# One sum bank at a time in the down phase, and score visits of seven banks

## The chip, the cores and the metric

The kernel runs on one core of a Trainium2 chip. The core has five engines with a queue each: TensorE (PE, matrix products, with weight loads listed apart as PEld), VectorE (DVE), ScalarE (ACT), GpSimd (POOL) and SyncE (SP, which here only issues transfers). An engine takes its instructions in order and waits for the others by semaphores. Products are written to PSUM, which this kernel uses as eight banks of 512 float32 numbers for each of 128 partitions; here ACT and DVE read it, and POOL works on SBUF alone.

The metric is the device time of one execution, in microseconds (us).

## The reference

One layer on 2048 tokens of width 512. Attention and a gated feed-forward part run side by side on the same normalised input, and both are added to it.

```python
xn = _layernorm(x)                                     # [2048, 512]
q, k, v = (xn @ wqkv), split into 32 heads of width 16
scores = q k^T / 4, kept where 0 <= i - j < 256        # sliding window
A = softmax(scores) v, heads joined, @ wo
B = ((xn @ w_gate) * (xn @ w_up)) @ w_down             # hidden width 1792
return x + A + B
```

## The kernel before

**Chunks and stages.** The tokens are worked on in NCH = 4 chunks T of 512 tokens. For a chunk there are the projections (`proj_v`, `proj_qk`), the scores and the values of its attention, the gate and up products of 14 hidden blocks (`gate`, `up`; NF = 14), and the *down phase*: for each of four blocks b of 128 tokens, 14 products of `down` (L432) and four of `wo` (L438) are summed in one PSUM bank `psd`, and `store` (L448) adds them to x on DVE and sends the block out.

**Scores.** Four heads share a group c of 128 columns, as four strips e of 32 rows. A *step* is one entry of the list that `batches` makes: a few pieces (c, key block, first and last query block) that fill 512 columns, for four heads. There are 75 steps: 15 for chunk 0 and 20 for each later chunk, five for each c. `scores` (L317) writes a step into the tile S, four PSUM banks, one bank per head. The four heads use four different 32-row parts of TensorE (`tile_position=(32 * e, 0)`), so that four products run side by side. One ACT instruction (L323) exponentiates the four banks into an SBUF strip P; POOL cuts the far edge of the window out of P (`triangle`, L162), and DVE the near edge (`mask_diag`, L347). S is a single tile: the next step's products wait until the exponential has read it. I call one such excursion of TensorE from the 128-row products to the 32-row products and back a *score visit*.

**Values.** When the strips of a group c are all there, `values` (L370) multiplies them by V in 64 by 32 parts of TensorE into two accumulators, DVE turns them (L376), and `divide` (L385 to L392) divides by the row sums into OT, which `wo` reads.

**Banks.** PSUM is split into S (four banks) and the pool `ps_m` of four one-bank buffers in rotation, which holds everything else: projections, gate, up, accumulators and `psd`. A tile of `ps_m` waits for the reader of the tile four places before it.

**Order.** The order on each engine is written out by `run`. It goes through the 75 steps; after each step's scores it calls `fill`, which issues *fillers* (half a gate, half an up, two down products and so on, from the list made by `fillers`) until a planned amount, `upto`, is spent. The planned amounts rise evenly over all 75 steps, and the table SHIFT moves some of them. Fillers of a chunk T come in this order: gate and up of its first FIRST = 3 blocks, then the down phase of chunk T-1, then the other gates and ups, then the projections of chunk T+1. So the down phase of chunk T-1 is spread over seven steps of chunk T: "score visit, ten to fourteen down products, score visit, ...". PADS puts runs of no-ops between fillers of TensorE at two steps. `norms` (layer norm of chunk T+1, with a transpose by DMA on SP) is hung on five steps at the down phase. Values of two groups are due together at one step; their two divides come 8 and 24 units of spent TensorE time later (`pending`).

Of the kernel before, what the change touches and what calls it, by code (L numbers as in the profile page):

```python
# [24 lines left out]
FIRST = 3  # L25
GAP = 10.6
PAIRS = ((0,), (1,), (2,), (3,)), ((0, 1), (2, 3)), ((0, 1), (2, 3)), ((0, 1), (2,))
SHIFT = {20: -2, 21: -5, 22: -8, 23: -11, 24: -14, 26: -10, 27: -7, 28: -3, 62: 3, 63: 6, 64: 12, 66: 12, 67: 11, 68: 9, 69: 6, 70: 3}
PADS = {27: 120, 57: 146}
MASKED, FIRST_DIVIDE, SECOND_DIVIDE = 8, 8, 24  # L30
COPY = dict(act=2.8, dve=3.2)
EXP, MASK, BOTH, SUMS, DIVIDE, TURN, STATS = 8.7, 1.9, 3.4, 4.2, 8.2, 6.1, 4.2
# [2 lines left out]
class Kernel:  # L35
    def __init__(self, ctx, tc, x, wqkv, wo, wg, wu, wd, out):
        self.ctx, self.tc, self.nc = ctx, tc, tc.nc
        _, S, D = x.shape
        self.S, self.D, self.F = S, D, wg.shape[1]
        assert D == 512 and S % 512 == 0 and self.F % 256 == 0  # L40
        self.NT, self.NCH, self.NF = S // 128, S // 512, self.F // 128
        self.x_d, self.out_d = x.flatten_outer_dims(), out.flatten_outer_dims()
        self.w_d = dict(qkv=wqkv, o=wo, g=wg, u=wu, d=wd)

        def pool(name, bufs, **kw):
            return ctx.enter_context(tc.tile_pool(name=name, bufs=bufs, **kw))
# [79 lines left out]

    def keep_busy(self, n):

        ps = self.ps_m.tile([128, 128], F32, tag="M", name="wps")
        for _ in range(n):  # L130
            self.nc.tensor.matmul(ps[:], lhsT=self.idle[:], rhs=self.idle[:], start=True, stop=True)

# [66 lines left out]
    def norm_transpose(self, t, by_dma):  # L199

        nc = self.nc
        xn = self.xns.pop(t)
        T, b = divmod(t, 4)
        if b == 0:
            self.xnT[T] = self.chunk2.tile([128, 4, 4, 128], BF16, tag="xnT", name=f"xnT{T}")
        if by_dma:
            nc.sync.dma_start_transpose(out=self.xnT[T][:, b, :, :], in_=xn[:])
            return
        n = 2 if b == 0 else 4
        for lo in range(0, 4, n):  # L210
            ps = self.ps_m.tile([128, n, 128], BF16, tag="M", name="xTp")
            for k in range(n):
                nc.tensor.transpose(ps[:, k, :], xn[:, 128 * (lo + k):128 * (lo + k) + 128], self.ident[:])  # L213
            nc.scalar.activation(out=self.xnT[T][:, b, lo:lo + n, :], in_=ps[:], func=ACT.Copy)

    def bank(self, ks, name):

        self.open = 3 not in ks
        if 0 in ks:
            self.cur = self.ps_m.tile([128, 512], F32, tag="M", name=name)  # L220
        return self.cur

    def book(self, engine, took, ready=0):
# [79 lines left out]
                out.append(REST[c])  # L303
        return out

    def scores(self, T, pieces):

        nc = self.nc
        S = self.s_tiles.tile([128, 4, 512], F32, tag="S", name="S")
        P = self.ppool.tile([128, 4, 512], BF16, tag="P", name="P")  # L310
        col = 0
        for c, m, q0, q1 in pieces:
            U, j = divmod(8 * T + m, 8)
            keys, q, n = slice(128 * j, 128 * j + 128), 64 * q0, 64 * (q1 - q0 + 1)
            for e in range(4):
                rows = slice(32 * e, 32 * e + 32)
                nc.tensor.matmul(S[:, e, col:col + n], lhsT=self.K[U, c][rows, keys],  # L317
                                 rhs=self.Q[T, c][rows, q:q + n],
                                 start=True, stop=True, tile_position=(32 * e, 0),
                                 skip_group_check=True)  # L320
            self.parts.setdefault((T, c), []).append((P, col, m, q, n))
            col += n
        nc.scalar.activation(out=P[:, :, 0:col], in_=S[:, :, 0:col], func=ACT.Exp, scale=0.25)  # L323
        self.book("act", EXP)
        self.masked = self.free["act"]
        self.strips[(T, pieces)] = P
        for at in self.places(pieces, 4):
            for half in (slice(0, 64), slice(64, 128)):
                self.triangle(P[half, :, at:at + 64], False)

    def places(self, pieces, far):

# [18 lines left out]
    def values(self, T, c, accs=None):  # L351
# [1 line left out]

        nc = self.nc
        if accs is None:
            accs = [self.ps_m.tile([128, 512], F32, tag="M", name="acc") for _ in range(2)]
# [61 lines left out]
    def down(self, T, b, lo, hi, part=0):  # L418

        nc = self.nc  # L420
        self.open = True
        if lo == 0 and part == 0:
            if T == self.NCH - 1 and b == 3:
                last = self.ps_m.tile([128, 128], F32, tag="M", name="psd3")
                self.sums[b] = [(self.late[3][:, 0:384], 0, 384), (last[:], 384, 512)]
            elif T == self.NCH - 1 and b == 2:
                self.sums[b] = [(self.late[2][:], 0, 512)]
            else:
                self.sums[b] = [(self.ps_m.tile([128, 512], F32, tag="M", name="psd")[:], 0, 512)]
        for f in range(lo, hi):  # L430
            ps, c0, c1 = self.sums[b][part]
            nc.tensor.matmul(ps, lhsT=self.hT[T, f][:, 128 * b:128 * b + 128],  # L432
                             rhs=self.Wd[:, f, c0:c1], start=(f == 0), stop=False)
# [19 lines left out]
    def fillers(self):  # L453
# [54 lines left out]
        for T in range(NCH):  # L508
            if T:
                if T + 1 < NCH:  # L510
                    for i, fs in norms(T + 1, 0, 1).items():
                        self.beside[self.first[T, 0] + (4, 5, 6, 7, 8)[i]] = fs
# [11 lines left out]
        for b in range(4):  # L524
            down(T, b)
            if b < 3:
                wo(T, b, (0, 1, 2))
        return [(*o, None, None)[:4] for o in out]

    def run(self):  # L530
        self.xns, self.stats, self.sums = {}, {}, {}
# [17 lines left out]
        self.beside = {}  # L549
        work = self.fillers()  # L550
        total = sum(w[0] for w in work) - RESERVE + SCORES * len(steps)
        total += sum(VALUES + SECOND * (len(keys) - 1) for keys in due.values())
        spent, n = 0, 0
        self.free = dict(act=0, dve=0)
        valued, ready, pending = -1, -1, []

        def fill(upto, group):
            nonlocal spent, n
            while n < len(work):
# [3 lines left out]
                if spent + cost / 2 > upto and not any(  # L563
                        w[2] is not None and w[2] <= group for w in work[n:]):
                    break
                spent += cost
                self.now = spent
# [10 lines left out]
            self.divide(*key)  # L578
            ready = self.last[key]

        held = None
        for g, s in enumerate(steps):
            keys = due.get(g, [])
            self.pads += PADS.get(g, 0)
            if held is None:
                valued = ready
                fill(-1, g + len(keys) // 2)
                while len(keys) == 2 and self.open:
# [4 lines left out]
            upto = max(total * (g + 1) / len(steps) + SHIFT.get(g, 0), spent + GAP)  # L593
            if g in (1, 2):
                self.new_values()
            for i, key in enumerate(keys):
# [20 lines left out]
        self.ps_s.__exit__(None, None, None)  # L617
        late = self.ctx.enter_context(self.tc.tile_pool(name="ps_late", bufs=1, space=bass.MemoryType.PSUM))
# [16 lines left out]
        self.down(T, 3, 0, self.NF, 1)  # L635
        self.wo(T, 3, (0, 1, 2, 3), 1)
        self.store(T, 3, 1)


@with_exitstack  # L640
# [34 lines left out]
```

## Time and profile before

| | |
|---|---|
| device time, median of three | 263.19 us (263.17 to 263.84) |
| span of the profiled execution, first to last instruction | 261.3 us |
| time around that span (median less span; the profiled execution's own device time is not listed) | 1.9 us |
| busy: PE, DVE, ACT, POOL | 98%, 69%, 67%, 44% of the span |
| mean granted clock of TensorE | 0.999 of full speed |
| stretches with the three down phases | about 69 to 88, 132 to 151 and 195 to 215 us |

Busy time of an engine is the time in which an instruction of it runs. The chain of work that ended last is followed back from the last instruction; its shares say which engine the time goes through. In the lists, `out<-in` are the tiles' names, sizes are partitions x elements, `xN` counts instructions, and a bracket gives the idle time before an instruction and who ended it. Matrix products overlap: each of 128x512 lasts 380 ns in the record, but they start every 216 ns. A few per cent of the products have no record, and where one is missing the trace shows a gap of 0.2 us.

### The profile page before, as it was taken

To read this page: it belongs to the slowest core of one execution; us is meant where nothing else is said; L and a number is where in the kernel's file an instruction comes from. 1 tells how busy PE (TensorE), PEld (TensorE's weight loads), DVE (VectorE), ACT (ScalarE), POOL (GpSimd) and SP (SyncE) were. 2 spreads that over 40 slices of the span, in tenths; PEclk is the share of its full clock that TensorE was granted. 3 is DMA by queue.
4 is the path that set the end of the run, shared out by engine and by line. 5 is a ranking of instruction groups with operands and counts; after the bars stand their busy time and mean duration, and the time that the engine had idled before them with its cause. 6 is when DMAs were issued, how large, how long until landed. Compare 5 with 4: busy or idle time off the path is not lost.

```text
span 261.3 us, 7724 instructions
## 1 busy us (share of the span) xinstructions
PE 255.5 (98%) x3154; PEld 117.4 (45%) x3170; DVE 179.5 (69%) x357; ACT 176.4 (67%) x143; POOL 115.7 (44%) x278
## 2 busy tenths in 40 slices
PE   7999999999999999999999999999999999999995
PEld 7443444444344544344544454344544445444453
DVE  6687888879846597557974769767795235977344
ACT  3477688888757866678775567767787546787600
POOL 6225342425457644334456644544443451464600
PEclk9999999999999999999999999999999999999999
DMA  6999910120012300002001310001000100000002
GB/s 203 373 353 340 284 26 20 24 48 1 3 33 38 94 3 1 3 0 48 3 3 40 83 44 3 0 1 27 24 3 0 43 24 20 5 0 3 1 3 83
DMA packets 19427, 15.05 MB, mean 58 GB/s; under 512 B 7360, under 2 KB 19392, under 8 KB 19392
## 3 DMA queue, kind: packets, MB, share of 16 engines
q1 hardware_dynamic: 18848, 14.26, 18.6%
q8 instruction: 26, 0.43, 0.7%
q10 hardware_dynamic: 544, 0.30, 0.4%
q14 instruction: 9, 0.07, 0.1%
HBM read 9.70 MB, written 2.10 MB: 45 GB/s over the span
## 4 chain that ended last, share of the span: by engine, by line
PE 96%; DVE 1%; DMA 1%; issue 1%
PE gp L399 19%; PE up L410 19%; PE psd L432 17%; PE qkp L255 11%; PE S L317 10%; PE acc L370 7%; PE vp L243 5%; PE psd L438 5%; PE L L432 2%; DMA x<-in_A_x_dram 1%; DVE st L173 1%; PE L L438 1%; PE L L370 0%; PE xTp L213 0%; DVE xn L194 0%
## 5 line engine op out<-in xcount | busy, mean ns | idle before, releaser
L323 ACT ACTIVATE P<-S 128x2048 bf16<-128x2048 f32 x75 | 140.7, 1876 | 49.6 <-PE S L317 41.1
L162 POOL TENSOR_SCALAR_AFFINE_SELECT P<-P 64x256 bf16<-64x256 bf16 x224 | 99.4, 444 | 124.2 <-ACT P L323 109.0
L399 PE MATMUL gp<-xnT,Wg 128*128 128x512 bf16 x224 | 60.1, 380 | 0.0
L410 PE MATMUL up<-xnT,Wu 128*128 128x512 bf16 x224 | 59.1, 380 | 0.0
L415 DVE TENSOR_TENSOR hT<-up,gsb 128x512 bf16<-128x512 f32 x56 | 38.3, 685 | 18.4 <-PE up L410 13.1
L432 PE MATMUL psd<-Wd,hT 128*128 128x512 bf16 (+1 forms) x202 | 46.9, 369 | 0.8 <-issue 0.6
L347 DVE TENSOR_TENSOR P<-P,diag 128x512 bf16<-128x512 bf16 (+1 forms) x75 | 29.6, 394 | 5.9 <-ACT P L323 5.9
L432 PEld LDWEIGHTS <-hT 128*128 128x128 bf16 x238 | 21.3, 98 | 25.3 <-issue 3.5
L410 PEld LDWEIGHTS <-Wu 128*128 128x128 bf16 x224 | 20.4, 98 | 25.6 <-issue 3.3
L399 PEld LDWEIGHTS <-Wg 128*128 128x128 bf16 x224 | 20.3, 98 | 25.3 <-issue 3.3
L317 PE MATMUL S<-Q,K 32*128 32x320 bf16 (+4 forms) x720 | 29.8, 254 | 0.1
L255 PE MATMUL qkp<-xnT,Wqkv 128*128 128x512 bf16 x128 | 29.9, 380 | 0.0
L234 ACT ACTIVATE gsb<-gp 128x512 bf16<-128x512 f32 x38 | 22.3, 596 | 7.7 <-PE gp L399 6.9
L317 PEld LDWEIGHTS <-K 32*128 32x128 bf16 x720 | 10.3, 92 | 30.7 <-issue 30.3
L376 DVE STREAM_TRANSPOSE at<-acc 128x512 f32<-128x512 f32 x30 | 19.1, 688 | 6.5 <-PE acc L370 6.4
L448 DVE TENSOR_TENSOR x<-psd,x 128x512 bf16<-128x512 f32 (+1 forms) x15 | 9.7, 655 | 15.7 <-PE psd L438 15.7
L255 PEld LDWEIGHTS <-Wqkv 128*128 128x128 bf16 x128 | 11.7, 98 | 14.7 <-issue 1.8
L370 PE MATMUL acc<-P,VS 64*32 64x320 bf16 (+4 forms) x672 | 17.7, 253 | 0.0
L370 PE MATMUL acc<-P,V 64*32 64x320 bf16 (+4 forms) x672 | 17.5, 253 | 0.0
L370 PEld LDWEIGHTS <-V 64*32 64x32 bf16 x720 | 15.1, 91 | 2.3 <-issue 1.7
L243 PE MATMUL vp<-Wqkv,xnT 128*128 128x512 bf16 x60 | 14.9, 379 | 0.3 <-issue 0.2
L370 PEld LDWEIGHTS <-VS 64*32 64x32 bf16 x720 | 14.7, 91 | 0.6 <-issue 0.2
(54 smaller groups left out, 178.9 us busy)
## 6 DMA issues: line engine op xcount, KB each, us to landing
out_dram<-x SPq DMA_DIRECT2D x15, 128.0 KB, 1.9
Wg<-in_B_w_gate_dram SPq DMA_DIRECT2D x2, 896.0 KB, 10.9
Wu<-in_B_w_up_dram SPq DMA_DIRECT2D x2, 896.0 KB, 12.4
Wd<-in_B_w_down_dram SPq DMA_DIRECT2D x1, 1792.0 KB, 17.6
Wqkv<-in_A_wqkv_dram SPq DMA_DIRECT2D x3, 512.0 KB, 5.5
x<-in_A_x_dram SPq DMA_DIRECT2D x2, 512.0 KB, 8.3
VS<-V SPq DMA_DIRECT2D x6, 144.0 KB, 2.6
x<-in_A_x_dram SPq DMA_DIRECT2D x3, 256.0 KB, 6.7
```

What stands on the lines that cost most here:

```text
L162: nc.gpsimd.affine_select(out=v, in_=v, pattern=pattern + [[1 if diag else -1, 64]], compare_op=ALU.is_ge if diag else ALU.is_gt, fill=0.0 ...
L234: nc.scalar.activation(out=out, in_=in_, func=ACT.Copy)
L243: nc.tensor.matmul(ps[:], lhsT=self.xnT[T][:, b, k, :], rhs=self.Wqkv[:, k, 1024:1536], start=(k == 0), stop=(k == 3))
L255: nc.tensor.matmul(ps[:], lhsT=self.Wqkv[:, k, lo:lo + 128], rhs=self.xnT[T][:, :, k, :], start=(k == 0), stop=(k == 3))
L317: nc.tensor.matmul(S[:, e, col:col + n], lhsT=self.K[U, c][rows, keys], rhs=self.Q[T, c][rows, q:q + n], start=True, stop=True, tile_posit ...
L323: nc.scalar.activation(out=P[:, :, 0:col], in_=S[:, :, 0:col], func=ACT.Exp, scale=0.25)
L347: self.nc.vector.tensor_tensor(out=v, in0=v, op=ALU.min, in1=self.diag.unsqueeze(1).unsqueeze(1).to_broadcast([128, 4, n, 64]))
L370: nc.tensor.matmul(accs[par][32 * e:32 * e + 32, q:q + n], lhsT=v, rhs=P[rows, e, col:col + n], start=(i == 0), stop=(i == len(todo) - 1), ...
L399: nc.tensor.matmul(ps[:], lhsT=self.Wg[:, k, 128 * f:128 * f + 128], rhs=self.xnT[T][:, :, k, :], start=(k == 0), stop=(k == 3))
L410: nc.tensor.matmul(ps[:], lhsT=self.Wu[:, k, 128 * f:128 * f + 128], rhs=self.xnT[T][:, :, k, :], start=(k == 0), stop=(k == 3))
L415: nc.vector.tensor_tensor(out=self.hT[T, f][:], in0=ps[:], in1=self.gsb[:], op=ALU.mult)
L432: nc.tensor.matmul(ps, lhsT=self.hT[T, f][:, 128 * b:128 * b + 128], rhs=self.Wd[:, f, c0:c1], start=(f == 0), stop=False)
```

## The change

- `ps_m` becomes four pools of one bank each, which `m_tile` takes in turn.
- At three places, after step 2 of the chunks 1, 2 and 3, all PSUM pools are closed and the whole down phase of the chunk before is issued in one piece by the new `down_phase`. The eight banks are then one bank d for the sums of block b, three banks B, and the four banks S. Of b to b + 1, d and B change places at the ends of the four banks (d is bank 3, then 0, then 3, then 0).
- The phase takes seven steps with it (3 to 9 of the chunk). For each b `wide_scores` computes one *plain* step (3, 4, 5, 6) in S, and three of the twelve (step, head) pairs of the steps 7, 8 and 9 in B. The products come in two rounds: first the three pairs in B together with the plain step's head that is *short*, the one that the three pairs leave free, then the plain step's other three heads. B is exponentiated by one or two ACT instructions (a step's heads that lie together), S by one.
- Order within b: BEFORE = 8, 6, 6, 6 down products, the visit, the rest of the down products, `wo`, `store`.
- The fillers ahead of a down phase are all issued before it; the rest is spread evenly over the steps of each stage (`spread`); SHIFT is empty, and PADS moves its second run from step 57 to step 47 and from 146 to 178 no-ops. Pending divides are issued FLUSH = 12 units before the phase. Layer norms of the next chunk come one per b (`along`), and the last at step 11.

```diff
-SHIFT = {20: -2, 21: -5, 22: -8, 23: -11, 24: -14, 26: -10, 27: -7, 28: -3, 62: 3, 63: 6, 64: 12, 66: 12, 67: 11, 68: 9, 69: 6, 70: 3}
-PADS = {27: 120, 57: 146}
+SHIFT = {}
+PADS = {27: 120, 47: 178}
+BEFORE, LEAD, FLUSH = (8, 6, 6, 6), 5, 12
...
-        self.ps_m = pool("ps_m", 4, space=bass.MemoryType.PSUM)
-        self.ps_s = tc.tile_pool(name="ps_s", bufs=1, space=bass.MemoryType.PSUM)
-        self.s_tiles = self.ps_s.__enter__()
+        self.psum = []
+        self.usual_banks(0)
+    def open_banks(self, name, bufs=1):
+        p = self.tc.tile_pool(name=name, bufs=bufs, space=bass.MemoryType.PSUM)
+        self.psum.append(p)
+        return p.__enter__()
+    def close_banks(self, n):
+        for _ in range(n):
+            self.psum.pop().__exit__(None, None, None)
+    def usual_banks(self, at):
+        self.at_bank = at
+        self.m_banks = [self.open_banks(f"ps_m{i}") for i in range(4)]
+        self.s_tiles = self.open_banks("ps_s")
+    def m_tile(self, shape, dtype, name):
+        pool = self.m_banks[self.at_bank]
+        self.at_bank = (self.at_bank + 1) % 4
+        return pool.tile(shape, dtype, tag="M", name=name)
...
+    def score(self, T, pieces, e, bank):
+        out, col, rows = [], 0, slice(32 * e, 32 * e + 32)
+        for c, m, q0, q1 in pieces:
             U, j = divmod(8 * T + m, 8)
-            keys, q, n = slice(128 * j, 128 * j + 128), 64 * q0, 64 * (q1 - q0 + 1)
-            for e in range(4):
-                rows = slice(32 * e, 32 * e + 32)
-                nc.tensor.matmul(S[:, e, col:col + n], lhsT=self.K[U, c][rows, keys],
-                                 rhs=self.Q[T, c][rows, q:q + n],
-                                 start=True, stop=True, tile_position=(32 * e, 0),
-                                 skip_group_check=True)
-            self.parts.setdefault((T, c), []).append((P, col, m, q, n))
+            q, n = 64 * q0, 64 * (q1 - q0 + 1)
+            out.append((col, dict(out=bank[:, col:col + n], lhsT=self.K[U, c][rows, 128 * j:128 * j + 128],
+                                  rhs=self.Q[T, c][rows, q:q + n], tile_position=(32 * e, 0))))
             col += n
-        nc.scalar.activation(out=P[:, :, 0:col], in_=S[:, :, 0:col], func=ACT.Exp, scale=0.25)
-        self.book("act", EXP)
-        self.masked = self.free["act"]
-        self.strips[(T, pieces)] = P
+        return out
+    def score_products(self, work):
+        for _, kw in sorted(work, key=lambda w: w[0]):
+            self.nc.tensor.matmul(kw.pop("out"), start=True, stop=True, skip_group_check=True, **kw)
+    def exp(self, out, in_):
+        self.nc.scalar.activation(out=out, in_=in_, func=ACT.Exp, scale=0.25)
+    def mask_far(self, T, pieces):
+        P = self.strips[(T, pieces)]
         for at in self.places(pieces, 4):
             for half in (slice(0, 64), slice(64, 128)):
                 self.triangle(P[half, :, at:at + 64], False)
+    def scores(self, T, pieces):
+        S = self.s_tiles.tile([128, 4, 512], F32, tag="S", name="S")
+        P, col = self.strip(T, pieces)
+        self.score_products([w for e in range(4) for w in self.score(T, pieces, e, S[:, e])])
+        self.exp(P[:, :, 0:col], S[:, :, 0:col])
+        self.book("act", EXP)
+        self.masked = self.free["act"]
+        self.mask_far(T, pieces)
+    def wide_scores(self, T, pieces, extra, B):
+        S = self.s_tiles.tile([128, 4, 512], F32, tag="S", name="S")
+        short = ({0, 1, 2, 3} - {e for _, e in extra}).pop()
+        work = []
+        for i, (other, e) in enumerate(extra):
+            if (T, other) not in self.strips:
+                self.strip(T, other)
+            work += self.score(T, other, e, B[:, i])
+        work += self.score(T, pieces, short, S[:, short])
+        self.score_products(work)
+        i = 0
+        while i < 3:
+            other, e = extra[i]
+            n = 1
+            while i + n < 3 and extra[i + n][0] == other:
+                n += 1
+            self.exp(self.strips[(T, other)][:, e:e + n, :], B[:, i:i + n, :])
+            i += n
+        P, _ = self.strip(T, pieces)
+        self.score_products([w for e in range(4) if e != short for w in self.score(T, pieces, e, S[:, e])])
+        self.exp(P[:], S[:])
+        self.mask_far(T, pieces)
+        for other in {o: None for o, e in extra if e == 3}:
+            self.mask_far(T, other)
+    def down_phase(self, T, g):
+        s = self.steps
+        plain = [s[g + i][1] for i in range(4)]
+        split = [(s[g + 4 + i][1], e) for i in range(3) for e in range(4)]
+        late, high = None, 0 if self.at_bank == 0 else 1
+        self.close_banks(5)
+        for b in range(4):
+            for name in ("ps_b", "ps_d") if b % 2 != high else ("ps_d", "ps_b"):
+                tiles = self.open_banks(name)
+                if name == "ps_d":
+                    d = tiles.tile([128, 512], F32, tag="d", name="psd")
+                else:
+                    B = tiles.tile([128, 3, 512], F32, tag="B", name="B")
+            self.s_tiles = self.open_banks("ps_s")
+            self.sums[b] = [(d[:], 0, 512)]
+            self.down(T - 1, b, 0, BEFORE[b])
+            for f in self.along.pop((T, b), ()):
+                f()
+            if late:
+                self.mask_diag(T, late)
+            late, extra = plain[b], split[3 * b:3 * b + 3]
+            self.wide_scores(T, late, extra, B)
+            self.down(T - 1, b, BEFORE[b], self.NF)
+            for other, e in extra:
+                if e == 3:
+                    self.mask_diag(T, other)
+            self.wo(T - 1, b, range(4))
+            self.store(T - 1, b)
+            self.close_banks(3)
+        self.usual_banks(0 if high == 0 else 1)
...
+                        if i < 4:
+                            self.along[T, i] = [f for _, f in fs]
+                        else:
+                            self.beside[self.first[T, 0] + 11] = fs
                 gu(T, range(FIRST))
-                for b in range(4):
-                    down(T - 1, b)
-                    wo(T - 1, b, range(4))
-                    add(0, lambda T=T, b=b: self.store(T - 1, b))
+                out.append((None, T))
...
+        downs = {self.first[T, 0] + 3: T for T in range(1, NCH)}
+        def spread(g):
+            end = next((k for k in range(n, len(work)) if work[k][0] is None), len(work))
+            stop = min([k for k in downs if k >= g], default=len(steps))
+            cost = sum(w[0] for w in work[n:end]) - (RESERVE if end == len(work) else 0)
+            cost += SCORES * (stop - g)
+            cost += sum(VALUES + SECOND * (len(due[k]) - 1) for k in due if g <= k < stop)
+            return spent, cost, g, stop - g
...
+            if g in downs:
+                valued = ready
+                fill(10 ** 9, -1)
+                valued = ready
+                assert work[n] == (None, downs[g])
+                late = self.down_phase(downs[g], g)
+                n += 1
+                skip = set(range(g, g + 7))
+                base, cost, g0, count = spread(g + 7)
+                fill(spent + LEAD, -1)
+                self.mask_diag(downs[g], late)
+                continue
...
+            if g + 1 in downs:
+                fill(upto - FLUSH, g)
+                while pending:
+                    pending.pop(0)[1]()
```

More of the change, by code (lines that the diff above doesn't have):

```diff
@@ L127, in keep_busy @@
     def keep_busy(self, n):
-        ps = self.ps_m.tile([128, 128], F32, tag="M", name="wps")
+        ps = self.m_tile([128, 128], F32, "wps")
         for _ in range(n):
@@ L210, in norm_transpose @@
         for lo in range(0, 4, n):
-            ps = self.ps_m.tile([128, n, 128], BF16, tag="M", name="xTp")
+            ps = self.m_tile([128, n, 128], BF16, "xTp")
             for k in range(n):
@@ L219, in bank @@
         if 0 in ks:
-            self.cur = self.ps_m.tile([128, 512], F32, tag="M", name=name)
+            self.cur = self.m_tile([128, 512], F32, name)
         return self.cur
@@ L304, in batches, with strip @@
         return out
-    def scores(self, T, pieces):
-        nc = self.nc
-        S = self.s_tiles.tile([128, 4, 512], F32, tag="S", name="S")
+    def strip(self, T, pieces):
         P = self.ppool.tile([128, 4, 512], BF16, tag="P", name="P")
+        self.strips[(T, pieces)] = P
         col = 0
         for c, m, q0, q1 in pieces:
-            U, j = divmod(8 * T + m, 8)
-            keys, q, n = slice(128 * j, 128 * j + 128), 64 * q0, 64 * (q1 - q0 + 1)
-            for e in range(4):
-                rows = slice(32 * e, 32 * e + 32)
-                nc.tensor.matmul(S[:, e, col:col + n], lhsT=self.K[U, c][rows, keys],
-                                 rhs=self.Q[T, c][rows, q:q + n],
-                                 start=True, stop=True, tile_position=(32 * e, 0),
-                                 skip_group_check=True)
-            self.parts.setdefault((T, c), []).append((P, col, m, q, n))
-            col += n
-        nc.scalar.activation(out=P[:, :, 0:col], in_=S[:, :, 0:col], func=ACT.Exp, scale=0.25)
-        self.book("act", EXP)
-        self.masked = self.free["act"]
-        self.strips[(T, pieces)] = P
+            n = 64 * (q1 - q0 + 1)
+            self.parts.setdefault((T, c), []).append((P, col, m, 64 * q0, n))
+            col += n
+        return P, col
+    def score(self, T, pieces, e, bank):
+        out, col, rows = [], 0, slice(32 * e, 32 * e + 32)
+        for c, m, q0, q1 in pieces:
+            U, j = divmod(8 * T + m, 8)
+            q, n = 64 * q0, 64 * (q1 - q0 + 1)
+            out.append((col, dict(out=bank[:, col:col + n], lhsT=self.K[U, c][rows, 128 * j:128 * j + 128],
+                                  rhs=self.Q[T, c][rows, q:q + n], tile_position=(32 * e, 0))))
+            col += n
+        return out
[6 more added lines that the diff above has]
+        P = self.strips[(T, pieces)]
         for at in self.places(pieces, 4):
@@ new lines, in down_phase @@
+    def down_phase(self, T, g):
[28 more added lines that the diff above has]
+        self.usual_banks(0 if high == 0 else 1)
+        return late
@@ L355, in values @@
         if accs is None:
-            accs = [self.ps_m.tile([128, 512], F32, tag="M", name="acc") for _ in range(2)]
+            accs = [self.m_tile([128, 512], F32, "acc") for _ in range(2)]
         todo = self.parts.pop((T, c))
@@ L421, in down @@
         self.open = True
-        if lo == 0 and part == 0:
-            if T == self.NCH - 1 and b == 3:
-                last = self.ps_m.tile([128, 128], F32, tag="M", name="psd3")
+        if lo == 0 and part == 0 and T == self.NCH - 1:
+            if b == 3:
+                last = self.m_tile([128, 128], F32, "psd3")
                 self.sums[b] = [(self.late[3][:, 0:384], 0, 384), (last[:], 384, 512)]
-            elif T == self.NCH - 1 and b == 2:
+            elif b == 2:
                 self.sums[b] = [(self.late[2][:], 0, 512)]
             else:
-                self.sums[b] = [(self.ps_m.tile([128, 512], F32, tag="M", name="psd")[:], 0, 512)]
+                self.sums[b] = [(self.m_tile([128, 512], F32, "psd")[:], 0, 512)]
         for f in range(lo, hi):
@@ L511, in fillers @@
                     for i, fs in norms(T + 1, 0, 1).items():
-                        self.beside[self.first[T, 0] + (4, 5, 6, 7, 8)[i]] = fs
+                        if i < 4:
+                            self.along[T, i] = [f for _, f in fs]
+                        else:
+                            self.beside[self.first[T, 0] + 11] = fs
                 gu(T, range(FIRST))
-                for b in range(4):
-                    down(T - 1, b)
-                    wo(T - 1, b, range(4))
-                    add(0, lambda T=T, b=b: self.store(T - 1, b))
+                out.append((None, T))
                 gu(T, range(FIRST, NF))
@@ L527, in fillers @@
                 wo(T, b, (0, 1, 2))
-        return [(*o, None, None)[:4] for o in out]
+        return [o if o[0] is None else (*o, None, None)[:4] for o in out]
     def run(self):
@@ L548, in run @@
                 due[self.last[T, cs[-1]] + 3 - len(cs)] = [(T, c) for c in cs]
-        self.beside = {}
+        self.steps, self.beside, self.along = steps, {}, {}
         work = self.fillers()
-        total = sum(w[0] for w in work) - RESERVE + SCORES * len(steps)
-        total += sum(VALUES + SECOND * (len(keys) - 1) for keys in due.values())
         spent, n = 0, 0
@@ L555, in run @@
         valued, ready, pending = -1, -1, []
+        downs = {self.first[T, 0] + 3: T for T in range(1, NCH)}
[6 more added lines that the diff above has]
+            return spent, cost, g, stop - g
         def fill(upto, group):
             nonlocal spent, n
-            while n < len(work):
+            while n < len(work) and work[n][0] is not None:
                 cost, f, before, after = work[n]
@@ L563, in fill @@
                 if spent + cost / 2 > upto and not any(
-                        w[2] is not None and w[2] <= group for w in work[n:]):
+                        w[0] is not None and w[2] is not None and w[2] <= group for w in work[n:]):
                     break
@@ L579, in divide @@
             ready = self.last[key]
-        held = None
+        held, skip, late = None, set(), None
+        base, cost, g0, count = spread(0)
         for g, s in enumerate(steps):
+            if g in skip:
+                continue
[10 more added lines that the diff above has]
+                self.mask_diag(downs[g], late)
+                continue
             keys = due.get(g, [])
@@ L587, in run @@
                 fill(-1, g + len(keys) // 2)
-                while len(keys) == 2 and self.open:
+                while keys and g > self.first[1, 0] and self.open:
                     fill(spent + work[n][0] / 2, g)
@@ L592, in run @@
             self.scores(*s)
-            upto = max(total * (g + 1) / len(steps) + SHIFT.get(g, 0), spent + GAP)
+            upto = max(base + cost * (g + 1 - g0) / count + SHIFT.get(g, 0), spent + GAP)
             if g in (1, 2):
@@ L616, in run @@
         T = NCH - 1
-        self.ps_s.__exit__(None, None, None)
-        late = self.ctx.enter_context(self.tc.tile_pool(name="ps_late", bufs=1, space=bass.MemoryType.PSUM))
+        self.close_banks(1)
+        late = self.open_banks("ps_late")
         self.late = [late.tile([128, 512], F32, tag=f"L{i}", name=f"L{i}") for i in range(4)]
@@ L637, in run @@
         self.store(T, 3, 1)
+        self.close_banks(5)
 @with_exitstack
```

## The prediction

> **What bounds the kernel now.** I read the page's busy times and its chain first, then who waits for whom on PE, then the order of time on PE around a score visit, then DVE ahead of a down phase.
>
> ```profile
> PE 255.5 (98%) x3154; PEld 117.4 (45%) x3170; DVE 179.5 (69%) x357; ACT 176.4 (67%) x143; POOL 115.7 (44%) x278
> ...
> PE 96%; DVE 1%; DMA 1%; issue 1%
> ```
>
> TensorE carries 96% of the chain. Its list of waits, whole:
>
> ```profile
> PE wps L131 <- DVE warm L95: 1.0, 1, 1.0
> PE psd L432 <- issue: 0.6, 4, 0.2
> PE xTp L213 <- DVE xn L194: 0.3, 1, 0.3
> PE psd L438 <- issue: 0.2, 1, 0.2
> PE L L432 <- issue: 0.2, 1, 0.2
> PE vp L243 <- issue: 0.2, 1, 0.2
> ```
>
> After the first microseconds no product waits for another engine. The 0.2 us gaps by "issue" are missing records: counting the products in program order, the stretches that hold them last as long as those without (a visit and 14 products are 3.46 us in both). So PE's time is a sum of its products and of what it costs to change between forms, and only that sum and new waits matter. The price of a visit is in the order of time on PE (start, duration):
>
> ```profile
> 71.92 0.40 PE L317 MATMUL S<-Q,K 32*128 32x256 bf16 x8
> 72.25 1.04 PE L432 MATMUL psd<-Wd,hT 128*128 128x512 bf16 x4
> 73.12 1.03 PE L438 MATMUL psd<-Wo,OT 128*128 128x512 bf16 x4
> 73.99 1.46 PE L432 MATMUL psd<-Wd,hT 128*128 128x512 bf16 x6
> 75.38 0.40 PE L317 MATMUL S<-Q,K 32*128 32x192 bf16 x8
> ```
>
> From the visit's start to the next product are 0.33 us (71.92 to 72.25). The 14 products after it take 3.13, and 14 x 0.216 = 3.02, so another 0.11 is lost behind it. A visit costs **0.44 us**; visits of 12 products cost the same as visits of 8. A full-width product streams 512 columns in 0.216, and each of the four heads has 512 columns, side by side; so about 0.22 is work and 0.22 the change of form and back.
>
> **Part by part: the visits.** Products are the same before and after (in program order 720 of scores, 1440 of values, 1010 of the rest). Only the visits differ: 75 become 66, that is 7 in each of the three phases become 4. Removed: 3 x 7 x 0.438 = 9.20 us. Added: 12 visits with two rounds. The second round follows the first in the same form, which no row of before shows for scores. Bounds: bare streaming, 0.213; or a whole visit, 0.438. The nearest row is the values, where one group alone or two in succession are done in one excursion:
>
> ```profile
> 123.40 0.26 PE L370 MATMUL acc<-P,V 64*32 64x192 bf16 x4
> ...
> 125.80 0.40 PE L317 MATMUL S<-Q,K 32*128 32x192 bf16 x8
> ...
> 236.78 0.26 PE L370 MATMUL acc<-P,V 64*32 64x192 bf16 x4
> ...
> 238.06 0.61 PE L410 MATMUL up<-xnT,Wu 128*128 128x512 bf16 x2
> ```
>
> Two groups take 2.40, one 1.28. The second adds 1.12 for 5 x 512 columns, 0.224 per 512. I take 0.224, since that row too adds columns without a change of form. The products of a round are issued by their column, so a head's second piece never stands in front of another head's first, and 21 products per visit are fewer per microsecond than the 192 in 2.40. A visit is then 0.66, twelve are 7.94. **Gain: 1.25 us** (1.33 at bare streaming; a loss of 1.31 at a whole visit).
>
> A measured rule speaks against that. The Trainium skill, "TensorE: Matmul & The Clock Gate", section "Measured speedup vs the span model", gives 3.07 times for four 32-row products of 512 columns side by side, not four times. By it a round would be about 0.278 (an estimate from that page: 4 x 0.213 / 3.07), the visits 8.6, and the gain 0.6. The 0.44 of a visit here already holds any loss that comes once per excursion, and the row of the values shows 5% beyond streaming for what is added.
>
> **ACT.** Seven exponentials of 1.88 us (13.1) become, per phase, four of 1.88, two of 1536 columns, two of 512 and two of 1024. Between the rows 0.596 (512 columns) and 1.876 (2048), 1024 take 1.02 and 1536 take 1.45: 13.6 in all. It matters only where TensorE waits for it: the next visit writes S, so the exponential of S must be done. From the trace an exponential starts 0.51 after its visit (71.92 to 72.43) and one behind another starts 0.1 before the first one's end. Block 0: 0.51 + 1.45 + 1.88 - 0.1 = 3.7 after the visit's start; the next visit comes after 0.66 + 16 x 0.216 = 4.1. Blocks 1 and 2 have three exponentials: 0.51 + 0.60 + 1.02 + 1.88 - 0.2 = 3.8 against 0.66 + 18 x 0.216 = 4.55. All hidden, with 0.4 to spare at the tightest; without that cover each 0.1 beyond costs 0.1 per phase.
>
> **DVE and the banks inside the phase.** The bank that held d belongs to the next B, so `store` must have read it: block 0's `wo` ends 0.66 + 10 x 0.216 + 0.2 = 3.0 after the visit, the addition takes 0.68 (L448), 3.7 against 4.1. In blocks 1 and 2 the norm, two `mask_diag` and the statistics stand before the next store, and end before `wo` does (about 0.45 + 0.69 + 0.18 + 2 x 0.44 = 2.2 us of work in 4.5). POOL has at most eight edge cuts of 0.44 to 0.52 and one `ve`, `rs` pair (0.85) in a period of 4.5: it falls behind in block 2 by about 0.5 and catches up in block 3 (four cuts). The values after the phase need the last strip of c = 1 some 6.9 after block 3's visit, and POOL is done at 6.3. On SP the same transposes and stores are issued in the order of the blocks; TensorE needs the transposed input first in the next chunk's projections, which before come some 25 us after the phase (88 to 113).
>
> **Entering the phase: new waits.** The first B takes banks 0 to 2 and d bank 3, instead of the oldest of four. Bank 3 held the last gate, bank 0 the last up: d waits for ACT's copy of that gate, issued four products before, and B for DVE's product of the last up, eight down products before. Before chunk 1: the visit of step 2 starts at u, ACT still copies the gate before it until u + 0.8, exponentiates until u + 2.6, copies the last gate until u + 3.1; the phase's first product is due at u + 0.44 + 12 x 0.216 = u + 3.03. Wait: 0.06. Before chunks 2 and 3 the copy ends 0.05 ahead. There DVE decides. From the start of the two value groups TensorE reaches B after 2.40 + 0.33 + 3.13 + 0.33 + 4.86 = 11.05. DVE's list up to the last up, by the rows of the same stretch of before (the second half of it):
>
> ```profile
> 132.34 0.34 DVE L385 RECIPROCAL rz<-at 128x32 f32<-128x32 f32 x1
> 132.72 0.94 DVE L389 TENSOR_TENSOR on<-at,rz 128x512 bf16<-128x512 f32 x1
> 133.69 0.71 DVE L392 STREAM_TRANSPOSE OT<-on 128x512 bf16<-128x512 bf16 x1
> 134.32 0.38 DVE L347 TENSOR_TENSOR P<-P,diag 128x512 bf16<-128x512 bf16 x1
> 134.63 0.68 DVE L415 TENSOR_TENSOR hT<-up,gsb 128x512 bf16<-128x512 f32 x1
> ```
>
> Starts follow each other by 0.37 (`rz`), 0.73 to 0.97 (`on`), 0.63 (`OT`), 0.6 (a product, or a copy). Four turns from 1.35 to 3.80; Q copy to 4.41; mask 4.61; first divide 6.36 to 6.46; hT 6.94 to 7.04; mask 7.26 to 7.4; gate copy to 8.0; second divide 9.6 to 9.98; two hT, the last ending at 10.9 to 11.26. So nothing, or 0.2 us of wait; I take 0.10 for each of the two, the middle. New waits: 0.06 + 0.20 = **0.26 us**.
>
> **The rest.** 32 more no-ops (266 to 298): stretches with and without them have equal length (12 products and a visit 3.03 us at 106 us, among no-ops, and at 160 us, with none), so nothing. Moving fillers leaves products and excursions as they are; the spacing of visits outside the phases becomes 10 to 16 products, as before, while ACT needs about 2.4 us per visit there and gets at least 2.6. Closing an open sum before values changes no form.
>
> **Sum.** 261.33 - 9.20 + 7.94 + 0.26 = 260.3 us of span. The median is 1.86 above the profiled span (263.19 - 261.33): **262.2 us**.
>
> **Rivals.**
> 1. *The second round costs a whole visit* (for: every 32-row excursion in the trace has one round; against: 12 products cost no more than 8, and the values add at 0.224). 12 x 0.876 = 10.51: 263.19 + 1.31 + 0.26 = 264.8, slower. It decides from 0.306 per second round on, where the gain is gone: (9.20 - 0.26) / 12 - 0.438.
> 2. *The newest bank.* The last hT runs one DVE instruction later (0.7) than worked out, before all three phases, because POOL's cuts stretch DVE or a planned copy falls to it. For: `on` took 0.94 beside POOL, 0.69 elsewhere; against: 0.16 is all that this row shows. 3 x 0.7 - 1.25 = +0.85: 264.0, slower, from 0.42 a phase on.
> 3. *The exponentials end last.* If ACT starts on B only after round two (+0.22), with no overlap of neighbours (+0.1 to 0.2) and a late start of block 0, TensorE waits some 0.1 to 0.3 per phase: 262.5 to 263.1, no clear change.
> 4. *Nothing waits*, with 0.213 a round: 261.9.
>
> **How the numbers follow.** No change and a change can be told apart from about 0.3% on, 0.79 us here: below 262.40 is faster, above 263.98 slower. Forecast with rival 4: 0.63, its own range 261.8 to 262.8, some three quarters of it below 262.40; rival 3: 0.16; rival 2: 0.12, half of it above 263.98; rival 1: 0.09, with most of its mass above. Faster 0.48 + 0.03 = 0.51; slower 0.06 + 0.07, and 0.06 for waits not seen in any row, 0.19; the rest 0.30. The range holds the forecast, rival 3 and rival 2: 261.7 to 264.2.
>
> **What would show it.** PE: 66 visits, the twelve wide ones some 0.55 us from start to the next product instead of 0.33, and four of them to a phase of 18 products a block. The list of PE's waits would name DVE at B once or twice with 0.1 to 0.2 and ACT at `psd` or S not at all or with less than 0.1. ACT's exponential of S ends before the next wide visit starts. Wrong would be: a wide visit of 0.7 or more (rival 1), waits at B over 0.4 (rival 2), at S (rival 3), a lower granted clock, or PE idle after a visit with no releaser named.

## The result, and the profile after

| | before | changed | ratio, 95% interval |
|---|---|---|---|
| first comparison | 263.34 us | 262.70 us | 0.9977 (0.9967 to 0.9988) |
| again, on another occasion | 263.32 us | 262.69 us | 0.9973 (0.9964 to 0.9981) |

The change gains 0.6 us, a quarter of a per cent. Both intervals lie below 1, but the gain is below the 0.3% from which the prediction called a change clear. The forecast of 262.2 was 0.5 us too low; 262.7 lies in its range and in the likeliest case's own range (261.8 to 262.8). The prediction gave 0.51 to a time below 262.40; what came is the outcome to which it gave 0.30.

I have two profiles of the changed kernel. From the page of the first, the busy times and the chain; then its list of what TensorE waited for (us in total, times, longest):

```profile
span 261.2 us, 7759 instructions
...
PE 255.2 (98%) x3154; PEld 119.9 (46%) x3170; DVE 168.3 (64%) x342; ACT 183.4 (70%) x167; POOL 115.2 (44%) x278
...
PE 87%; DVE 8%; issue 2%; ACT 1%; DMA 1%; ACTq 1%
```

```profile
PE wps L150 <- DVE warm L114: 1.0, 1, 1.0
PE psd L532 <- issue: 0.5, 3, 0.2
PE S L349 <- ACT P L352: 0.4, 1, 0.4
PE L L532 <- issue: 0.2, 1, 0.2
```

TensorE is as busy as before, but its share of the chain has fallen from 96% to 87%, and DVE's has risen from 1% to 8%: somewhere a product now waits for DVE. The list of waits does not show where: a full-width product lasts 0.38 in the record and the next starts 0.216 after it, so a wait of 0.1 or 0.2 leaves hardly any idle time between them. I found the waits by taking TensorE's order of time apart: every stretch against 0.216 per full-width product, 0.11 behind a visit, and 0.33 or 0.55 for the visit itself. In the kernel before, nothing is left over from the first visit to the last. In the changed kernel this is what remains:

| place | left over, us |
|---|---|
| into the phase, before chunk 1, 2, 3 | 0.07, 0.18, 0.18 |
| the pair of values behind each phase (2.45 for 2.40) | 3 x 0.05 |
| second score visit of the kernel, first profile only (0.44 of it idle time in the list) | 0.50 |
| products behind the first pair after a phase, second profile only | 0.23 |

The second profile shows a wide visit and the entry before chunk 2, on PE and then on DVE (start, duration, operation):

```profile
70.94 0.23 PE L349 MATMUL B<-Q,K 32*128 32x128 bf16 x3
70.95 0.25 PE L349 MATMUL S<-Q,K 32*128 32x64 bf16 x2
71.01 0.33 PE L349 MATMUL B<-Q,K 32*128 32x64 bf16 x6
71.05 0.51 PE L349 MATMUL S<-Q,K 32*128 32x320 bf16 x10
71.49 1.47 PE L532 MATMUL psd<-Wd,hT 128*128 128x512 bf16 x6
...
132.35 1.89 PE L532 MATMUL psd<-Wd,hT 128*128 128x512 bf16 x8
134.36 0.23 PE L349 MATMUL B<-Q,K 32*128 32x128 bf16 x3
```

```profile
131.47 0.92 DVE L489 TENSOR_TENSOR on<-at,rz 128x512 bf16<-128x512 f32 x1
132.42 0.71 DVE L492 STREAM_TRANSPOSE OT<-on 128x512 bf16<-128x512 bf16 x1
133.06 1.25 DVE L515 TENSOR_TENSOR hT<-up,gsb 128x512 bf16<-128x512 f32 x2
```

The wide visit takes 0.55 from its start to the next product (70.94 to 71.49), where a plain one takes 0.33: the second round costs 0.22. At the entry, eight down products end 1.73 and a change of form 0.1 after 132.35, so B was due at 134.18. DVE's last product of the gates ends at 133.06 + 1.25 = 134.31, and B starts at 134.36.

Over all visits the means are 0.435 for a plain one and 0.651 for a wide one, with what is lost behind them. By these rows TensorE's sum is -21 x 0.435 + 12 x 0.651 + 0.43 + 0.15 = -0.74 us. The profiles agree: from the first visit's start to the last product's they are 0.26 and 0.52 shorter than before, 0.76 and 0.75 without the 0.50 and the 0.23.

The medians differ by 0.64 and 0.63 only, and two things outside this stretch belong to the account. At the very end, the last two semaphore instructions of POOL stand 0.37 apart in all nine profiles of the changed kernel and its variants, and 0.08 apart in both of the kernel before: the program closes 0.29 later, and why is open. At the start, the first visit began 0.15 earlier in the two profiles than before; in all eleven it begins anywhere from 13.3 to 14.4, so this is no property of the change.

### The profile page after: what moved, and what is told of

Same layout as the page of the kernel before. It is cut to its first block, busy times and chain, and to the rows that moved or that the text cites. A ratio compares the mean times of both kernels' runs of the same rounds, so it can differ in the third digit from the quotient of the medians.

```text
span 261.2 us, 7759 instructions
## 1 busy us (share of the span) xinstructions
PE 255.2 (98%) x3154; PEld 119.9 (46%) x3170; DVE 168.3 (64%) x342; ACT 183.4 (70%) x167; POOL 115.2 (44%) x278
## 4 chain that ended last, share of the span: by engine, by line
PE 87%; DVE 8%; issue 2%; ACT 1%; DMA 1%; ACTq 1%
PE up L510 17%; PE gp L499 17%; PE psd L532 15%; PE qkp L274 9%; PE S L349 7%; PE acc L470 6%; PE vp L262 5%; PE psd L538 5%; PE L L532 2%; DVE at L476 2%; DVE hT L515 1%; DVE on L489 1%; PE B L349 1%; DMA x<-in_A_x_dram 1%; DVE st L192 1%
## 5 line engine op out<-in xcount | busy, mean ns | idle before, releaser
L352 ACT ACTIVATE P<-S 128x2048 bf16<-128x2048 f32 x66 | 123.8, 1876 | 24.6 <-PE S L349 19.3
L499 PE MATMUL gp<-xnT,Wg 128*128 128x512 bf16 x224 | 59.1, 380 | 0.0
L253 ACT ACTIVATE gsb<-gp 128x512 bf16<-128x512 f32 x49 | 28.5, 596 | 9.6 <-PE gp L499 9.6
L352 ACT ACTIVATE P<-B 128x1536 bf16<-128x1536 f32 (+2 forms) x18 | 17.8, 1022 | 17.8 <-PE B L349 10.9
L349 PE MATMUL S<-Q,K 32*128 32x320 bf16 (+4 forms) x624 | 28.7, 255 | 0.4 <-ACT P L352 0.4
L349 PEld LDWEIGHTS <-K 32*128 32x128 bf16 x720 | 11.5, 92 | 27.8 <-issue 26.9
```

The lines of the kernel that those rows point to most:

```text
L253: nc.scalar.activation(out=out, in_=in_, func=ACT.Copy)
L349: self.nc.tensor.matmul(kw.pop("out"), start=True, stop=True, skip_group_check=True, **kw)
L352: self.nc.scalar.activation(out=out, in_=in_, func=ACT.Exp, scale=0.25)
L499: nc.tensor.matmul(ps[:], lhsT=self.Wg[:, k, 128 * f:128 * f + 128], rhs=self.xnT[T][:, :, k, :], start=(k == 0), stop=(k == 3))
```

## The experiments

My theory after the profile (A): nine excursions fewer are worth about 1.3 us (nine changes of form saved, about 2 us, less three more rounds of 0.22, 24 in the wide visits for 21 before), and the entries of the phases (0.43) and the values behind them (0.15) take back 0.58; the wait at the second score visit is an accident of single executions. Against it stood: that this last wait belongs to the change (B); that the entry waits are not DVE's; and that the gain comes from the order of the fillers or the no-ops, not from the excursions. Each experiment was timed beside the kernel before; "the changed kernel" is 262.69 us throughout. The runs come from three chips, on which the kernel before took 263.32, 263.46 and 263.28, so a difference to the changed kernel across chips may be off by 0.15 us or so.

**The changed kernel again.**

> The changed kernel itself, for comparison on the same chip. Theory A (nine excursions fewer give 1.29 us, waits at the phases' entries take back 0.43, the values after the phases 0.15): 262.45 to 262.55 where ACT's two early transfers cost nothing extra, 0.3 to 0.6 more in executions where they hold the first exponential up, as in the profile at 15.02. Theory B (that hold-up belongs to the change): nearly all executions at 262.7 to 263.1.

Measured: 262.69 us (262.46 to 263.38). The median lies between what A and B had said, at the edge of B. The profile decides against B: ACT's two early transfers were issued in 1.33 us instead of the 2.23 of the first profile, the first exponential started at 14.11 instead of 15.02, and the second visit did not wait; in the six profiles below that leave these transfers on ACT the issue takes 1.32 or 1.33 too. Even so this execution took 262.73; it had the 0.23 gap of the table instead. So single executions lose a few tenths in different places, and the hold-up of the first profile is one of these.

**One down product more ahead of the first wide visit.** The second wide visit gets one more too, so that the distance between the two stays.

```diff
-BEFORE, LEAD, FLUSH = (8, 6, 6, 6), 5, 12
+BEFORE, LEAD, FLUSH = (9, 7, 6, 6), 5, 12
```

> BEFORE = 9, 7, 6, 6: one more down product of 0.216 us ahead of B in block 0, with the distances between visits kept near 17 and 18 products. Theory A: the 0.18 us wait at B before chunks 2 and 3 is gone (the stretch between the visit of step 2 and the first wide visit becomes 0.108 + 23 x 0.216 = 5.08, without residue), 0.36 us faster than the changed kernel; the 0.07 before chunk 1 stays, since it stands ahead of the sums. Rival (the entry waits do not come from DVE's last product): the stretch becomes 5.26 and the time stays.

Measured: 262.29 us, ratio 0.9962 to the kernel before (0.9949 to 0.9976), 0.40 faster than the changed kernel. Its PE, before chunk 2:

```profile
133.10 2.10 PE L532 MATMUL psd<-Wd,hT 128*128 128x512 bf16 x9
135.14 0.23 PE L349 MATMUL B<-Q,K 32*128 32x128 bf16 x3
```

Nine products and the change of form are 9 x 0.216 + 0.1 = 2.04, and B starts 2.04 after the first: the wait is gone, and 0.40 is about twice 0.18. DVE's share of the chain falls back to 0%. The 0.07 before chunk 1 is still there, as expected. The entry waits before chunks 2 and 3 were DVE's last product.

**Two more.**

```diff
-BEFORE, LEAD, FLUSH = (8, 6, 6, 6), 5, 12
+BEFORE, LEAD, FLUSH = (10, 8, 6, 6), 5, 12
```

> BEFORE = 10, 8, 6, 6: a second product more ahead of B. Theory A (only the 0.18 wait was to be had, and one product of 0.216 covers it): the same as with one more, 262.2 to 262.4. Rival (DVE is later in most executions than in the profile): up to 0.2 faster than that.

Measured: 262.25 us, ratio 0.9957 (0.9944 to 0.9971): the same as with one more. Nothing else was to be had there. These two versions are the fastest of this study, about 1.1 us under the kernel before.

**The cover of the exponentials taken away.**

```diff
-BEFORE, LEAD, FLUSH = (8, 6, 6, 6), 5, 12
+BEFORE, LEAD, FLUSH = (12, 6, 6, 6), 5, 12
```

> BEFORE = 12, 6, 6, 6: twelve down products ahead of the first wide visit, and so only 12 instead of 16 between the first and the second. Theory A: the wait at B before chunks 2 and 3 is gone (0.36 us less), but the cover of the exponentials is too: the exponential of S ends 3.66 after the first wide visit's start, the second is due after 0.66 + 12 x 0.216 = 3.25, so TensorE waits about 0.4 for ACT at S in each of the three phases; in sum 0.8 to 1.0 slower than the changed kernel, 263.5 to 263.7. Rival (TensorE does not depend on the exponential's end there, as no wait was seen in the changed kernel): 262.3, as with one more down product.

Measured: 263.64 us, ratio 1.0002 (0.9989 to 1.0015), 0.95 slower than the changed kernel. PE at the second wide visit of the phase before chunk 2, and ACT ahead of it:

```profile
138.92 0.22 PE L349 MATMUL B<-Q,K 32*128 32x128 bf16 x3
139.30 0.26 PE L349 MATMUL S<-Q,K 32*128 32x256 bf16 x1 [0.16 <-ACT P L352]
```

```profile
136.03 1.45 ACT L352 ACTIVATE P<-B 128x1536 bf16<-128x1536 f32 x1 [3.24 <-DVE mv L193]
137.38 1.87 ACT L352 ACTIVATE P<-S 128x2048 bf16<-128x2048 f32 x1
```

The three heads in B start, and the fourth, in S, waits until the exponential is done (137.38 + 1.87 = 139.25, S at 139.30). That is 0.36 of what each phase loses. Another 0.09 to 0.14 is lost ahead of it: the sums of the second block take one of B's banks, and their first product starts at 137.53, when the exponential of B is done (136.03 + 1.45 = 137.48). In the changed kernel the exponential of S ends 3.66 to 3.71 after its visit and the next visit comes 4.1 after it, so the cover at this place is four tenths.

**Each wide visit made into two.**

```diff
-    def wide_scores(self, T, pieces, extra, B):
+    def wide_scores(self, T, pieces, extra, B, between):
...
         P, _ = self.strip(T, pieces)
+        between()
...
-            self.wide_scores(T, late, extra, B)
-            self.down(T - 1, b, BEFORE[b], self.NF)
+            self.wide_scores(T, late, extra, B, lambda: self.down(T - 1, b, BEFORE[b], BEFORE[b] + 2))
+            self.down(T - 1, b, BEFORE[b] + 2, self.NF)
```

> The changed kernel with two down products between the two rounds of each wide visit, so that each of the twelve becomes two excursions; all products, strips and exponentials stay. Theory A (an excursion costs 0.22 us beyond its products): 12 x 0.22 = 2.6 us slower than the changed kernel, 265.1 to 265.4, and about 1.9 slower than the kernel before. Rival (the gain comes from closing the sums early or from another order of the fillers, not from fewer excursions): less than 1 us slower than the changed kernel.

Measured: 265.19 us, ratio 1.0076 (1.0060 to 1.0093): 2.50 slower than the changed kernel, with the same products, strips, exponentials and banks. PE:

```profile
70.94 0.23 PE L349 MATMUL B<-Q,K 32*128 32x128 bf16 x3
...
71.27 0.60 PE L533 MATMUL psd<-Wd,hT 128*128 128x512 bf16 x2
71.81 0.40 PE L349 MATMUL S<-Q,K 32*128 32x64 bf16 x9
72.14 1.04 PE L533 MATMUL psd<-Wd,hT 128*128 128x512 bf16 x4
```

Each half costs 0.33 and 0.11 behind it (71.27 to 71.81 are two products of 0.216 and 0.11). Twelve excursions more are 2.50 us, 0.21 each. That is the price on which the change is built, shown by itself: the gain is in the number of excursions.

**ACT's two early transfers moved to SP.**

```diff
-        self.swap_halves(0, self.nc.scalar)
+        self.swap_halves(0, self.nc.sync)
```

> The changed kernel with the two transfers that swap the halves of chunk 0's values issued by SP instead of ACT. Theory A: ACT's first exponential starts 0.5 us after the first score visit in the profile, the 0.44 wait of the second visit is gone, and the median falls by 0.2 to 0.4 towards the fastest executions of the changed kernel, 262.45. Theory B (the half microsecond comes from the new pools or the order of the fillers): the second visit waits as before, and the median stays at 262.7.

Measured: 267.81 us, ratio 1.0172 (1.0155 to 1.0190): a failed experiment as to its time. ACT's first exponential did start 0.45 after its visit and the second visit did not wait, as A has it, but SP came to these transfers late. First SP's issues in order of time (start, duration), then PE at the first values, with its wait in brackets:

```profile
13.62 8.75 SPq L106 DMA_DIRECT2D Wo<-in_A_wo_dram  x4
22.42 1.94 SPq L108 DMA_DIRECT2D x<-in_A_x_dram  x3
27.12 1.36 SPq L172 DMA_DIRECT2D VS<-V  x2
```

```profile
32.70 0.26 PE L470 MATMUL acc<-P,VS 64*32 64x192 bf16 x4 [2.55 <-DMA VS<-V]
```

The values waited for the swapped halves, and some 5 us were lost between 29 and 40 us. The wait itself is about half of it: behind it the granted clock was 0.57 to 0.58 from 34 to 38 us, and 1.00 in the four microseconds on either side. What the hold-up on ACT costs on average was not measured.

**No no-ops.** The prediction put the no-ops at nothing. Here the changed kernel has none.

```diff
-PADS = {27: 120, 47: 178}
+PADS = {}
```

> The changed kernel without its 298 no-ops. Theory A (no-ops pass beside the products and cost nothing, and their absence neither): 262.4 to 262.8, no new gap on TensorE. Rival (they keep something in step, such as the supply of instructions around the dense values): gaps on TensorE with no engine named, together 0.5 us or more slower.

Measured: 267.47 us, ratio 1.0156 (1.0136 to 1.0176), **4.8 slower** than the changed kernel. Theory A fell here. PE in the pair of values at 123 us, then the list of waits, for the weight loads (PEld) and the products (us in total, times, longest):

```profile
125.12 0.40 PE L470 MATMUL acc<-P,VS 64*32 64x320 bf16 x7
127.09 0.28 PE L470 MATMUL acc<-P,VS 64*32 64x256 bf16 x1 [1.58 <-issue]
```

```profile
PEld L470 <- issue: 6.2, 12, 1.8
...
PE acc L470 <- issue: 3.5, 3, 1.6
```

TensorE stops in the middle of its densest work, 384 instructions in 2.4 us, with no engine to wait for. Three of the five pairs last 4.23, 4.12 and 3.03 us, the others 2.45. The three lose 4.1 us together; this execution took 266.91, 4.2 above the changed kernel. I counted where each pair starts in TensorE's list of instructions, modulo 256: the three start at 89, 113 and 169, the unharmed ones at 33 and 193. With the no-ops the five start at 33, 209, 233, 210 and 235, in the kernel before at 25, 209, 241, 25 and 235.

**The place moved, and the kernel before without no-ops.**

In the changed kernel:

```diff
-PADS = {27: 120, 47: 178}
+PADS = {27: 120, 47: 82}
```

> The changed kernel with 82 instead of 178 no-ops in the second run, 202 of 298. Counted in TensorE's list of instructions, the two pairs of value groups of 384 instructions behind it move from places 210 and 235 of a block of 256 to 115 and 139; the three before it stay. Theory S (instructions come in blocks of 256, and a pair of value groups runs dry when a block ends some 90 to 170 instructions into it, as at places 89, 113 and 169 without no-ops): these two pairs last 3.5 to 4.2 instead of 2.45 and 2.40, the other three 2.40 to 2.45, and the time is 2.5 to 3.5 above the changed kernel, 265.2 to 266.2. Rival (the number of no-ops matters, not the place): a third of the 4.8 that all of them are worth, 1.6, over all pairs.

In the kernel before:

```diff
-PADS = {27: 120, 57: 146}
+PADS = {}
```

> The kernel before without its 266 no-ops. The pairs of value groups then start at places 25, 89, 121, 161 and 225 of a block of 256 instructions. Theory S: the second, third and fourth run dry by 1.8, 1.7 and 0.6 to 0.8, as without no-ops in the changed kernel, 267.2 to 267.8; the no-ops are then worth the same in both kernels, and the gain is not from them. Rival (the kernel before needs its no-ops less, so part of the difference between the kernels is theirs): under 266.5 or over 268.5.

Measured, the first: 265.96 us, 3.3 above the changed kernel. The fourth and fifth pair, now at 115 and 139, last 4.12 and 4.08; the others keep 2.45, 2.40 and 2.45. So it is the place, not the number. PE in the fifth pair:

```profile
219.34 0.35 PE L470 MATMUL acc<-P,V 64*32 64x256 bf16 x6
221.07 0.28 PE L470 MATMUL acc<-P,V 64*32 64x256 bf16 x2 [1.38 <-issue]
```

The second: 268.55 us, 5.3 above the kernel before beside it, 0.7 above the highest that I expected: the three pairs at 89, 121 and 161 last 4.46, 4.01 and 3.71 (2.06, 1.61 and 1.31 too long, the last twice what I had set). By the rival's figure, over 268.5, this would count for a share of the no-ops in the difference between the kernels. The traces say otherwise: as timed, with no-ops, every pair lasts 2.40 to 2.45 in both kernels, so the gain of the change owes nothing to them beyond keeping this out.

## Why the prediction was right or wrong

- *TensorE bounds, its time is a sum.* Right. The price of an excursion (0.22 beyond its products) came back as 0.21 in an experiment of its own.
- *The second round, taken at 0.224.* Right: 0.217. Rival 1, a whole visit, is out. The prediction's 1.33 for bare streaming is a slip: 9.20 - 12 x (0.438 + 0.213) is 1.39, and rival 4 is then 261.8, not 261.9. The estimate from the Trainium skill ("TensorE: Matmul & The Clock Gate", "Measured speedup vs the span model", 3.07 times for four products side by side) would have made it 0.278 and the gain 0.6; no loss of this kind shows in a round added to an excursion. That the whole change came to 0.6 as well is a coincidence.
- *ACT hidden with 0.4 to spare at the tightest.* Right: 3.66 to 3.71 after the visit where I had 3.7; without the cover TensorE waited 0.45 to 0.5 a phase. Rival 3 did not happen, though 262.7 lies in its range (262.5 to 263.1): the time alone could not have told it from what did.
- *Into the phase: 0.06 + 2 x 0.10.* The 0.06 was 0.07. The 0.10 was the middle between 0 and 0.2, and 0.18 was measured twice: the term was mis-sized. The row that should have decided was on the page: `on` takes 0.94 beside POOL's cuts, and POOL is at work there; it took 0.92. The sign that I had named, DVE at B in the list of waits, did not come; the wait shows in the order of time alone. Rival 2 was this mechanism in a larger size and did not happen.
- *The values behind a phase cost what they did.* Missed, 0.05 each. Their strips are listed in another order there, and the same pairs in the old order keep 2.40; that the order of the pieces is the cause is argued, not tried.
- *The no-ops: nothing.* Right for the difference between these two kernels, wrong as a statement on no-ops. It held because all five pairs of the changed kernel begin at harmless places, which the prediction did not work out: in that it was lucky. I had compared stretches with and without them, which shows what they cost and not what they prevent.
- *The sum.* A gain of 1.25 - 0.26 = 0.99 was forecast; 0.64 was measured. In the traces the visits give 1.32, the entries take 0.43 (0.17 more than forecast) and the values 0.15, and the end of the program takes 0.29, which the prediction left out. That sum is 0.45; the other 0.2 of the measured gain is not assigned, and single executions differ by as much at their start. The remaining 0.15 of the half microsecond lies in the base: the forecast stands on 263.19, and the kernel before took 263.34 in the comparison. The losses thus came to 0.87 where 0.26 was forecast; that 262.7 still fell into the likeliest case's range is in part luck.

## What to carry to other kernels

On an engine that never waits, price an edit by counting changes of form and check the sum by an experiment that adds the same changes back. When banks are regrouped, the first user of the new group waits for the newest reader of the old one (0.18 us here), so give it a product or two more of other work, and read the durations of that reader from a stretch with the same neighbours. Fillers that seem to cost nothing may hold something in place: take them out once before calling them free, and look where in the list of instructions the densest runs begin.

## What the runs showed of the hardware

TensorE can run out of instructions. Around 384 of them in 2.4 us, a pair of value groups lost 0.6 to 2.1 us when it began at places 89 to 169 of the list modulo 256, and nothing at 193 to 241 or at 25 and 33. The changed kernel's page lists the transfers of instructions (packets, MB, share of the DMA engines' span):

```profile
q8 instruction: 26, 0.43, 0.7%
```

26 packets for some 6,600 instructions of TensorE are about one for every 256, and the runs without no-ops, with 6,340, have 25, so a supply in blocks of that size fits both the packets and the places.

The traces also show why pairs that begin at 89 to 169 are harmed and those from 193 on are not. In all eight pairs that lost time the stop stands at the same place of the list, 191 modulo 256, which is 278 to 358 instructions into the pair. So blocks end there, and a pair of 384 runs dry when two such ends fall into it, at the second one; pairs that begin at 193 to 241, at 25 or at 33 hold one end only. The block is late in the packets too: each stop ends 1.25 to 1.45 us after the packet before it has landed (in the pair at 123 us without no-ops the packet lands at 125.83 and TensorE goes on at 127.09), and in no profile does TensorE pass such a place sooner than 1.2 us after its packet. The 0.23 behind the first pair of the second profile ends at such a place as well, 1.46 after the packet.

The Trainium skill ("Runtime: NRT & Kernel Launch", "Instruction fetch mechanics") states such blocks, and that crossing from one to the next is mostly hidden. The runs agree with the first. Against the second they show 0.6 to 2.1 us for one crossing, where another came about 1.5 us before it.
